# A decoder block in one kernel: five 512-column products ahead of the first scores, and transfers held to four at a time

## The chip, the cores and the metric

The kernel runs on one core of a Trainium2 chip. A core has TensorE (PE in the profile; its weight loads are listed apart as PEld), VectorE (DVE), ScalarE (ACT), GpSimd (POOL), SyncE (SP), and 16 DMA engines between HBM and the on-chip memories SBUF and PSUM. The metric is the device time of one execution in microseconds; lower is better.

## The reference, cut to what matters

Chunked attention: 4 batches, 8 heads, 768 positions, head size 64. Each chunk of 32 queries sees 8 memory keys, the 16 positions on its left, itself and 8 on its right. The attention output, 3072 tokens of 512 numbers, goes through a two-layer network with a rational function between the layers.

```
scores = scale * np.matmul(q_c, k_full.transpose(0, 1, 3, 2))
scores = scores - np.max(scores, axis=-1, keepdims=True)
a = np.exp(scores)
a = a / (np.sum(a, axis=-1, keepdims=True) + 1e-09)
out[:, :, c_start:c_end] = np.matmul(a, v_full)
...
h = x @ w_in                                  # 512 -> 2048
P = a[0] + a[1] * h + a[2] * h2 + a[3] * h3
Q = 1.0 + np.abs(b[0]) * np.abs(h) + np.abs(b[1]) * h2
return ((P / (Q + 1e-06)) @ w_out)            # 2048 -> 512
```

The weights arrive as 64-bit floats; the kernel unpacks them to 32-bit ones itself.

## The kernel before

The 3072 tokens are six blocks of 512. For each block the attention of four head pairs is computed, then the two layers. Each large product is made of three matmuls, since every operand is split into a high and a low part. The order of the work at the start is written out by hand in the string `SEQ`, one token per step, and the scheduler is told to keep it (`pin`, and `keep_in_program_order` for the loads).

What matters here is the first 30 us. All loads go out on one queue, SyncE's, in the order of the program, through the helper `load`. Load 1 is a part of the weights (512 KB). Loads 2 and 3 bring queries and keys of head pair 0 of block 0 (token `q00`, two halves of 288 KB), loads 4 and 5 those of pair 2 (`q02`), 6 and 7 those of pair 1 (`q01`), 8 and 9 the values of pair 0 (`v00`, two halves of 256 KB), 10 and 11 `q03`, 12 weights, 13 the 24 bytes of parameters, 14 and 15 `v02`, 16 and 17 `v01`, 18 weights, 19 and 20 `q10`, 21 and 22 `v03`. The framework gives the loads eight semaphores in turn, `DMAHW0` to `DMAHW7`, so a load waits for the landing of the eighth ahead of it.

TensorE begins, in `begin`, with `WARM` products that nobody reads: 14 transposes of the 128x128 identity matrix (`warm_up`). Then, as `SEQ` has it, come the scores of pair 0 and pair 2 (`b00`, `b02`, in `att_scores`, 16 matmuls each on 32-column strips of the array), the transpose of the exponentials of pair 0 (`c00`, in `att_turn`), the scores of pair 1 (`b01`), the values of pair 0 (`d00`, in `att_values`), the scores of pair 3 (`b03`), and the transposes `c02` and `c01`, one after the other. Between scores and transposes a pair passes through VectorE (`att_max`, `att_less`), ScalarE (`att_exp`) and a small fill on GpSimd (`absent`). A 32-bit matmul of the program, unlike a transpose, stands in the trace as two MATMUL records: the 16 of one `att_scores` are 32 there.

Of the kernel before, what the change touches and what calls it, by code (L numbers as in the profile page):

```python
# [35 lines left out]
SUMS_PE = [(0, 0), (0, 2), (1, 0), (1, 1), (1, 2)]  # L36
HI_ACT = [3, 4, 6, 10, 11, 12, 13, 15, 17, 18, 20, 22, 23, 25]
XL_POOL = [(0, 0), (0, 2), (1, 0), (1, 1), (1, 2)]
WARM = 14
CLEAR = [("qk", 0, "vp"), ("qk", 3, "ap"), ("qk", 1, "pv"), ("qk", 2, "vv"), ("v", 1, "pa"), ("v", 2, "pv"), ("v", 0, "pp"), ("v", 3, "pp")]  # L40
LEAD = 22
WHEN = dict(b=0, m=1, x=2, c=2, z=3)
WAIT = 4
# [46 lines left out]
def attn_moe(ctx, tc, qk, vm, w, ab, out, seq):  # L90
    nc = tc.nc
    P = 128
# [26 lines left out]
    ident = const.tile([P, P], F32, name="ident")  # L119
# [21 lines left out]
    def pin(ins):  # L141
        if pinned[0]:
            tc.keep_in_program_order(ins)

    def load(dst, src, queue=nc.sync):
        ins = queue.dma_start(out=dst, in_=src)
        if in_order[0]:
            tc.keep_in_program_order(ins)

# [5 lines left out]
    def slot(s, name, dtype, words=4 * DM):  # L155
        qk_bufs.pop(s, None)
        return wp.tile([P, 4 * DM], dtype, name=name, tag=f"slot{s}")[:, :words]
# [4 lines left out]
    def w_load(kind, j):  # L162
        if kind == "in":
            raws[j] = slot(RAW_SLOTS[j], "w_raw", U32)
        if j < WHOLE:
            load(half(raws[j], kind), half(w_bits_of[j][:, :4 * DM], kind))
        elif kind == "in":
            load(raws[j], w_bits_of[j][:, :4 * DM])
# [49 lines left out]
    def clear(region, engine):  # L218
        if engine is nc.scalar:
            engine.copy(region, zero.broadcast_to(region.shape))  # L220
        else:
            engine.memset(region, 0.0)

    def load_qk(i, p, t, queue=nc.sync):
        u = unit.setdefault((i, p), {})
        u["q"], u["k"] = [], []
        for h in range(2):
            load(rows(t[:, h * NK:h * NK + NK + NQ], h), qk[i, p, h], queue)
        for c in range(NC):
            u["q"].append(t[:, NK + c * CHUNK:NK + (c + 1) * CHUNK])  # L230
            first = t[:, start_in(c):start_in(c) + KEYS]
            u["k"].append(bass.AP(first.tensor, first.offset, [list(first.ap[0]), [NK + NQ, 2], [1, KEYS]]))
# [392 lines left out]
    def plan(n, kind, i, p):  # L625
        att.setdefault((n, kind), []).append((i, p))

    units = [(i, p, base) for i in range(3, NBLK)
             for p, base in enumerate(BASES.get(i, [first[i] - LEAD + 4 * p for p in range(NPAIR)]))]
    went = []  # L630
# [28 lines left out]

    warm = ps_h.tile([P, 512], F32, name="warm", tag="h")  # L660

    def warm_up():
        pin(nc.tensor.transpose(out=warm[:, :P], in_=ident, identity=ident))  # L663

    def begin():
        pick = {"a": nc.scalar, "v": nc.vector, "p": nc.gpsimd}
        for name, n, who in CLEAR:
            engines = [pick[x] for x in who]
            if name == "qk":
                t = qk_bufs[QK_SLOTS[n]] = slot(QK_SLOTS[n], "qk", F32, 2 * NK + NQ)  # L670
                clear(t[:, :NK], engines[0])
                clear(t[:, NK + NQ:], engines[1])
            else:
                if n >= 2:
                    v_bufs[n] = slot(V_SLOTS[n - 2], "v_first", F32).rearrange("x (h n) -> x h n", h=2)
                for h in range(2):
                    clear(v_bufs[n][:, h], engines[h])
        for _ in range(WARM):
            warm_up()
        if SUMS_PE:  # L680
            pin(nc.vector.tensor_reduce(ones, ident.rearrange("p (w h) -> p h w", h=2), axis=AX.X, op=ALU.max))

# [10 lines left out]
    def hand(token):  # L693
# [11 lines left out]
        elif kind in single:  # L705
            if kind == "o":
                early[0] = False
            single[kind](following(kind))
        elif kind in convert:
            convert[kind](w_seq[done[kind]])  # L710
            done[kind] += 1
        elif kind == "q":
            att_load(i, p)
        elif kind == "v":
            if i < BLOCKWISE:
                load_v(i, p, v_bufs[p if i == 0 else p % 2])
            else:
                att_loadv(i, p)
        elif kind == "E":
            evac(*order[count["o"]], [int(where)])  # L720
        elif kind == "K":
            fetch()
        elif kind == "X":
            ps_early.close()
            ps_pairs.append(ctx.enter_context(tc.tile_pool(name="ps_pairs", bufs=1, space=bass.MemoryType.PSUM)))
        elif kind == "W":
            warm_up()
        elif kind == "Y":
            load(par[:1], ab)
        elif kind == "P":  # L730
            wide = warm[:, P:P + 6]
            pin(nc.tensor.matmul(wide, lhsT=lone, rhs=par[:1], start=True, stop=True))
            pin(nc.scalar.copy(par, wide))
            pin(nc.scalar.activation(bab, par[:, 4:6], AF.Abs))
        previous[0] = kind

    pinned[0] = True
    tc.cur_priority = 900
    begin()
    for token in SEQ.split():  # L740
        tc.cur_priority += 4
# [102 lines left out]
```

## Time and profile before

| | |
|---|---|
| median of 3 runs | 599.34 us (598.25 to 599.51) |
| profiled execution, its own time | 598.73 us |
| its span in the trace | 596.9 us, so 1.8 us lie around it |
| PE busy | 586.8 us, 98% of the span |
| DVE, ACT, POOL busy | 78%, 67%, 68% |

The table says that TensorE is the engine that is nearly never idle; where its few idle times lie is read from the chain of waits and the timeline. Times below are from the start of the span.

### The profile page before, as it was taken

The numbers are of one execution on the slowest core, as the hardware profiler recorded it, in microseconds if no ns is written. First come the engines' busy times: TensorE is split into PE (matmuls) and PEld (weight loads), VectorE is DVE, ScalarE is ACT, GpSimd is POOL, SyncE is SP. The second block draws the span as 40 slices with busy tenths as digits, with TensorE's granted clock in tenths as the row PEclk, the third lists the DMA queues.
The fourth block names the chain that finished last, engine by engine and source line by source line (L and its number), as shares of the span: only waits on it lengthen the run. The fifth ranks groups of instructions, "written<-read, shape, count | busy, mean of one in ns | idle before, by whom it ended". The sixth has DMA issues, their size and how long they took to land.

```text
span 596.9 us, 13088 instructions
## 1 busy us (share of the span) xinstructions
PE 586.8 (98%) x5111; PEld 478.4 (80%) x5111; DVE 464.9 (78%) x762; ACT 401.9 (67%) x665; POOL 406.4 (68%) x376
## 2 busy tenths in 40 slices
PE   7899999999999999999999999999999999999997
PEld 6677888888787878878888888888888888888886
DVE  5899999898797759888877778787787766666673
ACT  4699999898667655656566666565765656755673
POOL 5468998798546766576677576766667677667682
PEclk9999999999999999999999999999999999999999
DMA  8965346230345344332331422312510100100001
GB/s 304 406 206 213 146 177 212 72 128 13 124 131 165 98 151 127 94 111 72 99 87 50 154 43 87 94 36 81 178 36 1 37 10 9 71 1 1 0 1 70
DMA packets 34591, 61.14 MB, mean 102 GB/s; under 512 B 4066, under 2 KB 20706, under 8 KB 34146
## 3 DMA queue, kind: packets, MB, share of 16 engines
q1 hardware_dynamic: 34386, 60.18, 30.6%
q8 instruction: 40, 0.66, 0.5%
q14 instruction: 21, 0.17, 0.1%
q10 hardware_dynamic: 144, 0.13, 0.1%
HBM read 44.56 MB, written 7.34 MB: 87 GB/s over the span
## 4 chain that ended last, share of the span: by engine, by line
PE 95%; DVE 2%; ACT 1%; DMA 1%; issue 0%; SPq 0%; POOL 0%; DVEq 0%
PE h L489 44%; PE o L504 43%; PE pairs L315 2%; PE pairs L293 2%; PE pa L428 1%; PE pa L361 1%; DMA qk<-in_qk_dram 1%; PE pa L412 1%; PE pa L454 0%; DVE e L379 0%; PE pa L434 0%; ACT e L396 0%; DVE ct L602 0%; ACT eT L419 0%; PE warm L663 0%
## 5 line engine op out<-in xcount | busy, mean ns | idle before, releaser
L489 PE MATMUL h<-x_hi,w_hl 128*128 128x512 f32 x768 | 240.3, 394 | 0.4 <-DVE ct L602 0.3
L504 PE MATMUL o<-w_hl,ghi 128*128 128x512 f32 x768 | 236.8, 390 | 0.0
L566 POOL TENSOR_TENSOR cy<-cy,ha 128x512 f32<-128x512 f32 x96 | 124.6, 1298 | 140.4 <-ACT cy L562 135.8
L504 PEld LDWEIGHTS o<-w_hl,ghi 128*128 128x128 f32 x768 | 143.9, 188 | 29.8 <-ACT v_main L546 0.2
L489 PEld LDWEIGHTS h<-x_hi,w_hl 128*128 128x128 f32 x768 | 141.7, 188 | 32.4 <-DVE ct L602 1.1
L489 PE MATMUL h<-x_lo,w_hl 128*128 128x512 f32 x384 | 150.0, 391 | 0.2 <-POOL x_lo L467 0.2
L504 PE MATMUL o<-w_hl,glo 128*128 128x512 f32 x384 | 150.0, 391 | 0.0
L614 POOL TENSOR_TENSOR glo<-ct,ghi 128x512 fp32r<-128x512 f32 x95 | 122.9, 1294 | 9.1 <-ACT ghi L609 3.2
L594 DVE SCALAR_TENSOR_TENSOR ct<-ct,par,h 128x512 f32<-128x512 f32 x82 | 61.2, 746 | 56.2 <-ACT h L590 55.5
L575 DVE TENSOR_TENSOR ct<-ct,h 128x512 f32<-128x512 f32 x96 | 65.6, 684 | 39.4 <-ACT ct L571 37.8
L586 ACT ACTIVATE h<-cy 128x512 f32<-128x512 f32 x82 | 49.1, 599 | 69.5 <-DVE ct L579 56.1
L557 ACT ACTIVATE ha<-h 128x512 f32<-128x512 f32 x96 | 57.4, 598 | 54.4 <-PE h L489 54.3
L607 POOL TENSOR_TENSOR ghi<-ct,zero 128x512 fp32r<-128x512 f32 x81 | 84.2, 1040 | 2.5 <-PE o L504 1.2
L504 PEld LDWEIGHTS o<-w_hl,glo 128*128 128x128 f32 x384 | 72.1, 188 | 16.8 <-POOL glo L614 1.6
L489 PEld LDWEIGHTS h<-x_lo,w_hl 128*128 128x128 f32 x384 | 72.1, 188 | 16.1 <-POOL x_lo L467 0.6
L562 ACT ACTIVATE cy<-ha,bab 128x512 f32<-128x512 f32 x96 | 78.4, 817 | 2.6
L571 ACT ACTIVATE ct<-h,par 128x512 f32<-128x512 f32 x96 | 73.6, 766 | 5.6 <-PE h L489 5.5
L579 DVE SCALAR_TENSOR_TENSOR ct<-ct,par,h 128x512 f32<-128x512 f32 x96 | 71.6, 746 | 3.0
L602 DVE SCALAR_TENSOR_TENSOR ct<-h,ct 128x512 f32<-128x512 f32 x82 | 56.5, 689 | 2.6
L598 DVE SCALAR_TENSOR_TENSOR h<-cy,h 128x512 f32<-128x512 f32 x82 | 56.5, 689 | 0.0
L590 ACT ACTIVATE h<-h 128x512 f32<-128x512 f32 x82 | 47.7, 582 | 2.6
L204 POOL TENSOR_TENSOR w_hl<-w_raw,w_hl 128x512 fp32r<-128x512 f32 x32 | 42.0, 1318 | 6.4 <-ACT w_hl L199 5.7
(80 smaller groups left out, 461.9 us busy)
## 6 DMA issues: line engine op xcount, KB each, us to landing
w_raw<-in_w_dram SPq DMA_DIRECT2D x26, 512.0 KB, 5.9
qk_pairs<-in_qk_dram SPq DMA_DIRECT2D x16, 576.0 KB, 4.2
v_main<-in_vm_dram SPq DMA_DIRECT2D x16, 512.0 KB, 5.1
out_dram<-v_main SPq DMA_DIRECT2D x23, 256.0 KB, 2.3
qk<-in_qk_dram SPq DMA_DIRECT2D x16, 288.0 KB, 5.8
eT<-blocks SPq DMA_DIRECT2D x64, 64.0 KB, 2.1
xf<-blocks SPq DMA_DIRECT2D x64, 64.0 KB, 2.1
v_main<-in_vm_dram SPq DMA_DIRECT2D x12, 256.0 KB, 6.4
```

The costliest lines, as they stand in the source:

```text
L489: pin(nc.tensor.matmul(h, lhsT=wt[:, cols], rhs=xt[i][:, ct, :], start=ct == m == 0, stop=ct == NCT - 1 and m == 2))
L504: ins = nc.tensor.matmul(o, lhsT=gt[:, cols], rhs=wt, start=begin and m == 0, stop=end and m == 2)
L557: pin(nc.scalar.activation(c["ha"], c["h"], AF.Abs))
L562: pin(nc.scalar.activation(c["y"], c["ha"], AF.Identity, scale=B1, bias=B0))
L566: pin(nc.gpsimd.tensor_tensor(c["y"], c["y"], c.pop("ha"), op=ALU.mult))
L571: pin(nc.scalar.activation(c["t"], c["h"], AF.Identity, scale=A3, bias=A2))
L575: pin(nc.vector.tensor_tensor(t, t, h, op=ALU.mult))
L579: pin(nc.vector.scalar_tensor_tensor(t, t, A1, h, op0=ALU.add, op1=ALU.mult))
L594: pin(nc.vector.scalar_tensor_tensor(t, t, A0, r, op0=ALU.add, op1=ALU.mult))
L598: pin(nc.vector.scalar_tensor_tensor(r, yy, QC, r, op0=ALU.add, op1=ALU.mult))
L607: pin(nc.gpsimd.tensor_tensor(ghi, chain[z]["t"], zero.broadcast_to([P, TB]), op=ALU.add))
L614: pin(engine.tensor_tensor(glo, chain.pop(z)["t"], gh[z].bitcast(F32), op=ALU.subtract))
```

## The change

The constant `WARM` goes from 14 to 5, and `begin` calls `warm_wide` in place of `warm_up`: a real 32-bit matmul of the identity with the identity repeated four times, 512 columns, into the same PSUM tile. The calls of `warm_up` that `SEQ` makes later (token `W`) stay. In `load`, each of loads 5 to 40 gets a dependency on the load four ahead of it, so that SyncE issues it only when that one has landed.

```diff
-WARM = 14
+WARM = 5
+AHEAD = 4
+PACED = 40
...
+    sent = []
+
     def load(dst, src, queue=nc.sync):
         ins = queue.dma_start(out=dst, in_=src)
+        sent.append(ins.ins)
+        if AHEAD < len(sent) <= PACED:
+            tc.add_manual_dep(ins.ins, sent[-1 - AHEAD].name, mybir.DependencyInfo(mybir.DependencyClass.Sync, mybir.DependencyReason.DATA), reason="pace")
...
+    def warm_wide():
+        pin(nc.tensor.matmul(warm.rearrange("p (b n) -> p b n", n=P), lhsT=ident, rhs=ident.unsqueeze(1).broadcast_to([P, 4, P]), start=True, stop=True))
+
...
         for _ in range(WARM):
-            warm_up()
+            warm_wide()
```

The first place is the start of TensorE's program, before and after the change; `warm` is the unread tile, `pa` a tile of scores, and the brackets name the semaphores waited for.

```order
L663 MATMUL warm<-ident 128x128 [waits Pool_49]
L663 MATMUL warm<-ident 128x128 x13
L361 MATMUL pa<-qk 32x128 [waits DMAHW1_49,DMAHW2_49,DVE_49,Pool_49]
L361 MATMUL pa<-qk 32x128 x15
L361 MATMUL pa<-qk 32x128 [waits DMAHW4_49,DMAHW3_49,DVE_49]
```

```order
L670 MATMUL warm<-ident 128x512 [waits Pool_49]
L670 MATMUL warm<-ident 128x512 x4
L368 MATMUL pa<-qk 32x128 [waits DMAHW1_49,DMAHW2_49,DVE_49,Pool_49]
L368 MATMUL pa<-qk 32x128 x15
L368 MATMUL pa<-qk 32x128 [waits DMAHW4_49,DMAHW3_49,DVE_49]
```

Nothing moved: the five wide products stand where the 14 transposes stood, and the scores behind them have the same waits. On all engines but SyncE the rest of the order and the waits are the same as before.

The second place is loads 4 to 16 in SyncE's program, before and after; `qk_120` is `q02`, `qk_117` is `q01`, `v_main0_102` is `v00`, `qk_114` is `q03`, `v_first_125` is `v02`, `v_main1_103` is `v01`.

```order
L146 DMA qk_120<-in_qk_dram 64x1152 [waits DVE_49] x2
L146 DMA qk_117<-in_qk_dram 64x1152 [waits Pool_49]
L146 DMA qk_117<-in_qk_dram 64x1152
L146 DMA v_main0_102<-in_vm_dram 64x1024 [waits Pool_49]
L146 DMA v_main0_102<-in_vm_dram 64x1024 [waits DMAHW0_49,Pool_49]
L146 DMA qk_114<-in_qk_dram 64x1152 [waits DMAHW1_49,Activation_49]
L146 DMA qk_114<-in_qk_dram 64x1152 [waits DMAHW2_49]
L146 DMA w_raw_148<-in_w_dram 128x1024 [waits DMAHW3_49]
L146 DMA par_93<-in_ab_dram 1x6 [waits DMAHW4_49]
L146 DMA v_first_125<-in_vm_dram 64x1024 [waits DMAHW5_49]
L146 DMA v_first_125<-in_vm_dram 64x1024 [waits DMAHW6_49,DVE_49]
L146 DMA v_main1_103<-in_vm_dram 64x1024 [waits DMAHW7_49]
```

```order
L150 DMA qk_120<-in_qk_dram 64x1152 [waits DVE_49]
L150 DMA qk_120<-in_qk_dram 64x1152 [waits DMAHW0_49,DVE_49]
L150 DMA qk_117<-in_qk_dram 64x1152 [waits DMAHW1_49,Pool_49]
L150 DMA qk_117<-in_qk_dram 64x1152 [waits DMAHW2_49]
L150 DMA v_main0_102<-in_vm_dram 64x1024 [waits DMAHW3_49,Pool_49]
L150 DMA v_main0_102<-in_vm_dram 64x1024 [waits DMAHW4_49,Pool_49]
L150 DMA qk_114<-in_qk_dram 64x1152 [waits DMAHW5_49,Activation_49]
L150 DMA qk_114<-in_qk_dram 64x1152 [waits DMAHW6_49]
L150 DMA w_raw_139<-in_w_dram 128x1024 [waits DMAHW7_49]
L150 DMA par_93<-in_ab_dram 1x6 [waits DMAHW0_49]
L150 DMA v_first_125<-in_vm_dram 64x1024 [waits DMAHW1_49]
L150 DMA v_first_125<-in_vm_dram 64x1024 [waits DMAHW2_49,DVE_49]
```

The order of the loads is the same; what moved is the semaphore waited for: load 5 now waits for load 1 (`DMAHW0`), where before the first load to wait for load 1 was load 9.

## Rows read from the trace of the kernel before

**Rows 1.** The page: busy time, and PE's granted clock in 40 slices (9: 90% or more).

```profile
PE 586.8 (98%) x5111; PEld 478.4 (80%) x5111; DVE 464.9 (78%) x762; ACT 401.9 (67%) x665; POOL 406.4 (68%) x376
...
PEclk9999999999999999999999999999999999999999
```

**Rows 2.** Whom TensorE's matmuls waited for, whole run: us, times, longest.

```profile
PE pa L361 <- DMA qk<-in_qk_dram: 2.0, 1, 2.0
...
PE pa L412 <- issue: 1.2, 1, 1.2
```

**Rows 3.** The chain that ended last, 0 to 18 us: start, us, what.

```profile
2.19 4.35 DMA qk<-in_qk_dram
...
8.67 0.70 DVE mx L369
...
10.98 0.66 PE pa L412 x4
...
16.34 1.13 issue
```

**Rows 4.** Timeline of the matmuls: start, us, line, out<-in, count, idle before.

```profile
1.44 3.25 PE L663 MATMUL warm<-ident 128*128 128x128 f32 x14 [1.44 <-POOL ident masks.py:199]
6.68 3.64 PE L361 MATMUL pa<-qk 128*32 128x128 f32 x64 [1.99 <-DMA qk<-in_qk_dram]
...
11.78 1.08 PE L361 MATMUL pa<-qk 128*32 128x128 f32 x32
...
17.47 0.60 PE L412 MATMUL pa<-ident,e 128*128 128x128 f32 x4 [1.20 <-issue]
...
18.43 1.08 PE L428 MATMUL pa<-v_first,eT 128*32 128x128 f32 x32
...
25.09 1.08 PE L428 MATMUL pa<-v_first,eT 128*32 128x128 f32 x32 [0.15 <-ACT eT L419]
```

**Rows 5.** Matmul groups, 1 to 10.5 us, then 10.9 to 20: busy us, mean ns.

```profile
L361 PE MATMUL pa<-qk 128*32 128x128 f32 x64 | 3.6, 420 | 2.0 <-DMA qk<-in_qk_dram 2.0
...
L361 PE MATMUL pa<-qk 128*32 128x128 f32 x64 | 2.2, 275 | 0.0
```

**Rows 6.** Packets, MB: 4-15, 15-15.1, 0-65.2, 65.2-66.3, 0-115.3, 115.3-116.4 us.

```profile
q1 hardware_dynamic: 1105, 3.92, 98.2%
...
q8 instruction: 1, 0.02, 62.8%
...
q8 instruction: 6, 0.10, 0.6%
...
q8 instruction: 1, 0.02, 5.2%
...
q8 instruction: 8, 0.13, 0.4%
...
q8 instruction: 1, 0.02, 5.5%
```

**Rows 7.** Busy us (and records) of PE, PEld, DVE, ACT, POOL in three stretches.

```profile
0.00:15.00 15.00, 10.91 (x202) 9.51 (x206) 8.31 (x15) 6.01 (x8) 8.21 (x21) 1.00 0.87 304
...
0.00:65.30 65.30, 59.07 (x839) 47.54 (x840) 56.03 (x101) 50.45 (x88) 42.04 (x58) 1.00 0.78 291
0.00:115.40 115.40, 109.17 (x1088) 88.68 (x1089) 101.81 (x174) 97.17 (x167) 86.02 (x93) 1.00 0.62 224
```

**Rows 8.** Issue to landing: loads 2 to 5; 15 to 17; 36 and 37.

```profile
DMA to landing us min/median/max: 4.3/4.4/4.4
...
DMA to landing us min/median/max: 6.7/6.7/6.8
...
DMA to landing us min/median/max: 2.9/2.9/2.9
```

**Rows 9.** Timeline of VectorE around 19 us.

```profile
18.25 0.68 DVE L324 TENSOR_REDUCE sums<-e 128x8 f32<-128x512 f32 x1
19.92 0.17 DVE L334 TENSOR_SCALAR rinv<-pa 128x8 f32<-128x8 f32 x1 [0.98 <-PE pa L434]
```

## The prediction

> **What bounds the kernel now.** I read the page first. TensorE is busy 98% of the span [rows 1], so whatever TensorE loses or wins early is likely to arrive at the end undiminished. Next, whom TensorE waits for over the whole run. Only two idle times there exceed 1 us: 2.0 us before the first scores, ended by the landing of queries and keys, and 1.2 us before a transpose, ended by nothing that the profile shows ("issue") [rows 2]. Both lie in the first 18 us, and both are on the chain that ended last [rows 3]. The two halves of the change aim at this stretch, so the question is what each does to these two places.
>
> The first place. Load 3 is issued at 2.19 and lands 4.35 later, at 6.54 [rows 3]. The scores of pairs 0 and 2 start at 6.68, 64 records that take 3.64 us [rows 4], and VectorE takes the maximum of the first pair from 8.67 [rows 3]. From there the chain runs through VectorE, ScalarE and GpSimd to the transpose at 10.98, so 2.31 us behind the maximum [rows 3]. In these early scores a record takes 420 ns on average, in the scores after 10.9 us only 275 [rows 5]; 32 of the later ones take 1.08 us, 64 of the early ones 3.64 [rows 4]. The page prints a granted clock of full speed in every slice [rows 1], but these durations say that the early scores ran at the lower level (1.2 GHz) and the later ones at the upper (2.4 GHz). The 14 transposes ahead of them, 3.25 us of work, with 1.99 us of idle time behind [rows 4], did not bring the clock up. It came up somewhere between 10.32, the end of the early scores (6.68 + 3.64), and 10.98, so 3.64 to 4.30 us after real matmuls began.
>
> The second place. From 16.34 TensorE stands for 1.13 us with all its inputs there [rows 3], and goes on at 17.47 [rows 4]. I read this as TensorE out of instructions, for these reasons. In 4 to 15 us the DMA engines carry loads alone, 1105 packets, 98% of their time; the first packet of 0.02 MB of queue 8, kind "instruction", starts between 15.0 and 15.1 [rows 6]. By then TensorE has 202 matmuls and 206 weight loads behind it, 408 records [rows 7]. The seventh packet starts at about 65.3 and the ninth at about 115.4 [rows 6], with 839 + 840 = 1679 and 1088 + 1089 = 2177 records done [rows 7]: a packet for each (2177 - 1679) / 2 = 249 records. At that pace the first one was due at 1679 - 6 x 249 = 185 records. TensorE gets there inside the scores that begin at 11.78, since 14 transposes, 64 scores, a transpose of four and two warm-up ones make 84 matmuls with as many weight loads, 168 records, ahead of them. So the packet was due at about 11.9 and began at 15.0, 3.1 us late, and TensorE went on 2.4 us after that, at 17.47. The loads issued at that time took 6.7 us from issue to landing; two alone on the queue took 2.9 [rows 8]. The 3.8 us between are queueing, near enough to 3.1 to be the same queue.
>
> **The wide products.** Removed are 14 transposes; 14 of them take 3.25 us, the last of them for some 0.42 after it started [rows 4, 5], so (3.25 - 0.42) / 13 = 0.217 us for 128 columns at the lower level. A real matmul stands as two records, as the 32 scores of a pair for the 16 of the program. How long a 512-column record of 32-bit data takes, no row shows. Upper bound: four times the 128-column transpose, 0.87 us; the scores support it, (3.64 - 0.42) / 15 = 0.215 for each round of four strips of 128 columns [rows 4, 5]. Lower bound: nothing, if the products ended before the queries land at 6.54. I take the upper bound, since the scores are the same kind of matmul. Five products are then 5 x 2 x 0.87 = 8.7 us at the lower level and end at 1.44 + 8.7 = 10.1 if the clock never comes up, and half of what is left goes once it does. With the clock up as long after the first real matmul as before, 3.64 to 4.30 us, it rises at 5.1 to 5.7, and the products end in the middle between that and 10.1: 7.6 to 7.9. That is later than the landing at 6.54, so the first scores now wait for their own warm-up instead of for data. They then run at the upper level: 1.08 us for 32 records [rows 4] and some 0.02 to VectorE, so the maximum begins at 8.7 to 9.0 instead of 8.67. **Term 1: +0.2 us** (0.0 to 0.3). The bounds are wider. With shorter products or an earlier clock, the maximum begins at 6.68 + 1.1 = 7.8: -0.9. If the clock does not rise until the products end, it begins at 10.1 + 1.1 = 11.2: +2.5. The scores of pair 2 behind them get faster too, but the transpose at 10.98 waits for the chain and not for them; that gain is nothing.
>
> **The pacing.** SyncE executes nothing but loads in this stretch, so what is queued behind a waiting load is the next loads alone. Loads 1 to 4 go as before. Load 5 now goes when load 1 has landed, and from there each fourth load follows a landing. A transfer alone takes 2.9 us [rows 8]; with 3 others ahead it took 4.4 in the bunch of loads 2 to 5 [rows 8]. So four in flight queue between 0 and 1.5 us, where eight queued 3.8. The instruction packet, due at 11.9 + 0.2, then begins at 12.1 to 13.6, and with the same 2.4 us behind it TensorE has its instructions by 14.5 to 16.0, before the 16.34 + 0.2 at which it needs them. The whole 1.13 us would go. What is late next is VectorE, which finishes its sum at 18.25 + 0.68 = 18.93 and idles for 0.98 until TensorE releases it at 19.92 [rows 9]; with TensorE earlier by more than that, VectorE sets the pace. **Term 2: -1.0 us** (0 to -1.1).
>
> What the pacing may cost: the landing of later loads. The tightest are the values `v02`, loads 14 and 15, read at 18.43 [rows 4], or at 18.43 - 1.1 + 0.2 = 17.5 after the change. Load 15 follows 11, 11 follows 7, and 7 follows 3, so it lands at 6.54 + 3 L, L being issue to landing with four in flight. At 2.9 it is 15.2, at 3.65 it is 17.5, at 4.4 it is 19.7. I take an L of 3.3, since the bunch of loads 2 to 5 started behind a load of twice the size and a steady flow of four does not bunch: cover of about 1 us, **term 3: 0** (0 to +3.7, below).
>
> The sum goes against the profiled execution's own 598.73: 598.73 + 0.2 - 1.0 = **597.9 us**. That execution is 0.6 below the median of the runs shown, 599.34; its clock came up just where the first transpose began, and a run with a later rise pays for it in the work from 10.98 on, which the change would spare. I do not add this.
>
> The Trainium skill, "DMA: Bandwidth & Descriptors", section "Queues, rings and completion order", says that a DMA engine goes round-robin over the queue rows it has work for, packet by packet. By that rule an instruction packet never waits behind the whole queue of loads, a shorter queue would not bring it sooner, and the sum would be that of rival B. The 3.1 us of delay above speak against it here, but they are inferred from counts.
>
> **The rivals.** A, the forecast: 597.9.
>
> B: the gap at 16.34 stays. The packet may be late for another reason than the loads' queue, or the idle time may be no lack of instructions at all. For it: the profile names no releaser for the gap, and only one execution is seen. Against it: delay and queueing agree (3.1 and 3.8). Time: 598.73 + 0.2 = 598.9.
>
> C: the pacing starves TensorE. For it: L was 4.4 when four were in flight [rows 8]. Then `v02` lands at 19.7 and TensorE waits 2.2 us for it; `v03`, load 22, follows load 2 (landed a transfer ahead of load 3, about 5.9) by five rounds, 5.9 + 5 x 4.4 = 27.9, where it is read at 25.09 [rows 4] - 1.1 + 0.2 + 2.2 = 26.4, another 1.5. Time: 597.9 + 3.7 = 601.6. It begins to cost at an L of 3.65, and decides the sign from about 4.1. Against it: 2.9 for a transfer alone, and that the DMA engines were nearly saturated by loads before as well, so that fewer in flight lose little.
>
> D: the first scores come with the data, from shorter products or an early clock: 598.73 - 0.9 - 1.0 = 596.8. It needs products that end by 6.7, so less than 5.2 us for the five.
>
> E: the clock rises only after the products: 598.73 + 2.5 - 1.0 = 600.2.
>
> **How the numbers follow.** A 0.50, B 0.20, C 0.10, D 0.14, E 0.06. I predict A's 597.9, with a range of its own of 597.2 to 598.6. A measurement of this kernel tells about 0.2%, 1.2 us, from no change: faster is below 598.1, slower above 600.5. Of A about two thirds lie below 598.1 (0.33), with D 0.47 faster; the rest of A, B, and E make 0.43; C makes 0.10. The range reaches from D's 596.8 to E, 600.0, and leaves out C, half of E and the edge of D.
>
> **What would show it.** Right: five products as ten records ending at 7.6 to 7.9, the maximum of pair 0 at 8.7 to 9.0; scores at the later duration (275 ns) from the start; loads 5 to 20 at 3 to 3.6 us from issue to landing; the first instruction packet by 13.6; no "issue" gap of 1 us around 16; `v02` landed before TensorE asks. Wrong: the gap is still there with its packet at 15 (B), TensorE waiting for a load between 12 and 26 us (C), products that take 5 us or 8.7 (D, E).

## The result and the profile after

The changed kernel takes 602.74 us, median of 8 runs (601.25 to 605.21), against 599.16 for the kernel before on the same chip: ratio 1.0058, 95% interval 1.0044 to 1.0073, so 3.5 us slower. The prediction was 597.9 us, in a range up to 600.0. The profiled execution took 602.7, with a span of 600.8 us.

The page of the profile after differs little from [rows 1]; what differs shows in whom TensorE's matmuls waited for over the whole run (us in total, times, longest), to be held against [rows 2]. (From `load` on, line numbers are 7 higher than before, from `warm_wide` on 10.)

```profile
PE 589.0 (98%) x5107; PEld 476.8 (79%) x5107; DVE 465.1 (77%) x762; ACT 401.8 (67%) x665; POOL 406.3 (68%) x376
```

```profile
PE pa L368 <- DMA qk<-in_qk_dram: 1.7, 2, 1.2
...
PE pa L435 <- DMA v_first<-in_vm_dram: 1.5, 2, 0.9
...
PE pa L435 <- DMA v_main<-in_vm_dram: 1.2, 2, 0.7
```

The reader is to see that the row with "issue" is gone, that the wait of 2.0 us ahead of the first scores is gone too, and that six waits for loads stand in their place, 4.4 us in all (1.7 + 1.5 + 1.2). The timeline of the matmuls after says where the early work and four of the six stand (compare [rows 4]):

```profile
1.44 6.49 PE L670 MATMUL warm<-ident 128*128 128x512 f32 x10 [1.44 <-POOL ident masks.py:199]
7.86 1.96 PE L368 MATMUL pa<-qk 128*32 128x128 f32 x64
11.31 0.66 PE L419 MATMUL pa<-ident,e 128*128 128x128 f32 x4 [1.50 <-POOL e L399]
...
16.01 1.40 PE L419 MATMUL pa<-ident,e 128*128 128x128 f32 x8
...
18.39 1.08 PE L435 MATMUL pa<-v_first,eT 128*32 128x128 f32 x32 [0.55 <-DMA v_first<-in_vm_dram]
...
20.83 1.08 PE L435 MATMUL pa<-v_main,eT 128*32 128x128 f32 x32 [0.73 <-DMA v_main<-in_vm_dram]
...
25.74 1.23 PE L368 MATMUL pa<-qk 128*32 128x128 f32 x32 [1.17 <-DMA qk<-in_qk_dram]
27.91 1.08 PE L435 MATMUL pa<-v_first,eT 128*32 128x128 f32 x32 [0.94 <-DMA v_first<-in_vm_dram]
```

The products run to 7.9 us and the 64 early scores behind them take 1.96 us, where they took 3.64. The transposes `c02` and `c01` run from 16.01 without the gap between them, behind which `c01` stood at 17.47. At the values `v02` nothing is left of that: 18.39 against 18.43. Then four waits for loads follow one another. VectorE's first maximum, in the timeline of that engine after, is 0.34 us later than in [rows 3]:

```profile
9.01 0.69 DVE L376 TENSOR_REDUCE mx<-pa 128x8 f32<-128x512 f32 x1 [4.23 <-PE pa L368]
```

The loads of the kernel after, grouped by time of issue (4 to 7 us, 13 to 14.5, 17 to 17.9, 18.5 to 20; the last column is us from issue to landing, as in [rows 8]):

```profile
qk<-in_qk_dram SPq DMA_DIRECT2D x3, 288.0 KB, 3.6
...
v_first<-in_vm_dram SPq DMA_DIRECT2D x2, 256.0 KB, 4.2
...
v_main<-in_vm_dram SPq DMA_DIRECT2D x2, 256.0 KB, 2.9
...
qk<-in_qk_dram SPq DMA_DIRECT2D x2, 288.0 KB, 5.9
```

Most loads land sooner than before, but fewer are on the way, and the flow stops twice. SyncE's timeline of the kernel after (start of the first load, us to the end of the last issue, number of loads):

```profile
13.07 1.82 SPq L150 DMA_DIRECT2D v_first<-in_vm_dram  x2
17.02 1.11 SPq L150 DMA_DIRECT2D v_main<-in_vm_dram  x2
18.18 0.59 SPq L150 DMA_DIRECT2D w_raw<-in_w_dram  x1
18.88 1.50 SPq L150 DMA_DIRECT2D qk<-in_qk_dram  x2
20.65 4.10 SPq L150 DMA_DIRECT2D v_first<-in_vm_dram  x2
```

Behind load 15 (issued at 14.4) nothing goes out until load 16 at 17.02: it waits for load 12, which is 512 KB of weights and took 5.2 us. Behind load 21 (20.65) load 22 goes only at 24.3: it waits for load 18, weights too, which took 6.0. After each stop the engines nearly stand still: from 17.2 to 18.2 us their busy share is 0.04, from 24.2 to 25.5 it is 0.16. The windows of both kernels, before first and after second, show what that makes of the flow (window; its length; busy us and records of PE, PEld, DVE, ACT, POOL; granted clock; DMA share; GB/s):

```profile
10.00:20.00 10.00, 8.14 (x223) 6.68 (x215) 7.43 (x15) 5.92 (x11) 1.60 (x4) 1.00 1.00 384
20.00:30.00 10.00, 9.62 (x131) 6.95 (x130) 9.25 (x20) 7.00 (x15) 5.40 (x7) 1.00 1.03 407
30.00:45.00 15.00, 14.44 (x299) 11.49 (x297) 14.66 (x27) 13.95 (x25) 9.18 (x12) 1.00 0.62 203
```

```profile
10.00:20.00 10.00, 8.00 (x215) 6.63 (x215) 7.84 (x16) 6.00 (x11) 1.61 (x4) 1.00 0.78 253
20.00:30.00 10.00, 7.16 (x119) 5.37 (x119) 6.69 (x16) 4.70 (x11) 3.60 (x4) 1.00 0.79 261
30.00:45.00 15.00, 13.66 (x198) 9.96 (x200) 14.09 (x24) 13.31 (x24) 9.36 (x14) 1.00 0.85 292
```

Between 10 and 30 us the loads come at 253 and 261 GB/s where they came at 384 and 407; after 30 us the paced kernel still brings what the other already has. Its TensorE, VectorE and ScalarE all do less in 20 to 30 us. As a mark for the whole start I take the first product of the second layer, before and after, from the timelines:

```profile
52.00 0.61 PE L504 MATMUL o<-w_hl,ghi 128*128 128x512 f32 x2
```

```profile
55.92 0.61 PE L511 MATMUL o<-w_hl,ghi 128*128 128x512 f32 x2
```

It starts 3.92 us later, and the span is 600.8 - 596.9 = 3.9 us longer. The loss is complete before the second layer begins.

### The profile page after: what moved, and what is told of

It is laid out like the page before. It is cut to its first block, busy times and chain, and to the rows that moved or that the text cites. A ratio compares the mean times of both kernels' runs of the same rounds, so it can differ in the third digit from the quotient of the medians.

```text
span 600.8 us, 13082 instructions
## 1 busy us (share of the span) xinstructions
PE 589.0 (98%) x5107; PEld 476.8 (79%) x5107; DVE 465.1 (77%) x762; ACT 401.8 (67%) x665; POOL 406.3 (68%) x376
## 4 chain that ended last, share of the span: by engine, by line
PE 91%; DMA 6%; POOL 1%; DVE 1%; ACT 1%; issue 0%; SPq 0%; POOLq 0%
PE o L511 43%; PE h L496 43%; DMA v_main<-in_vm_dram 2%; PE pairs L322 2%; DMA w_raw<-in_w_dram 2%; PE pairs L300 2%; DMA qk<-in_qk_dram 1%; DMA v_first<-in_vm_dram 1%; PE pa L435 1%; POOL v_main L229 0%; POOL qk L229 0%; POOL v_first L229 0%; PE pa L461 0%; PE pa L419 0%; PE pa L368 0%
```

## The experiments

The theory after this result: pacing at four makes the loads too slow, rival C of the prediction. Against it stood two others: that the wide products cost the time (a late first chain), and that the paced flow is tied to the slowest of the 16 DMA engines. Each kernel is the changed kernel with the edit shown; ratios are to the kernel before on the same chip. Its medians there run from 598.76 to 599.21 us, so kernels of different experiments are best compared by their ratios.

**The products alone.**

```diff
-PACED = 40
+PACED = 0
```

> Wide products alone, no pacing. Theory S (four loads in flight starve TensorE; the wide products cost 0.3 us): within 0.5 us of before, about 599.4, with the gap of 1.1 us near 16 us still there and the first instruction packet at about 15. Rival W (the wide products cause the loss): above 601, and no wait of TensorE for loads after the first scores.

Measured: 599.4 us, ratio 1.0003 [0.9990, 1.0017]. That is what theory S had. The products by themselves cost nothing that can be told, so they do not explain the loss. TensorE's timeline of this kernel:

```profile
18.11 0.60 PE L461 MATMUL pa<-ident,xt 128*128 128x128 f32 x4 [1.25 <-DVE e L386]
```

A gap of 1.25 us is still there. It stands behind the transposes `c01`, where it stood ahead of them: four matmuls with their four weight loads later, 8 records. The change puts 5 products (10 matmul records and as many weight loads) where 14 transposes (28 records in all) stood, so exactly 8 fewer. A gap that keeps its place by the count of records is what a lack of instructions gives. The packet of queue 8 begins at 15.7 us, TensorE goes on 2.4 later, as before. The row names an instruction of VectorE, but in the changed kernel the same transposes run at 17.24, ahead of that instruction (17.41 there), so they do not need it.

**The pacing alone.**

```diff
-WARM = 5
+WARM = 14
...
-            warm_wide()
+            warm_up()
```

> Pacing alone, 14 transposes. Theory S: slower by 3 us or more, about 602.4 (the changed kernel less 0.3), TensorE waiting 4 to 5 us in all for loads between 17 and 45 us, no 1 us gap near 16. Rival W: within 1 us of before, or faster by the 1.0 of the gap.

Measured: 601.33, ratio 1.0039 [1.0027, 1.0051], so 2.3 us of the 3.5. The direction is that of theory S; its 602.4 us and its 4 to 5 us of waits were too high. The waits for loads:

```profile
PE pa L368 <- DMA qk<-in_qk_dram: 3.4, 3, 2.0
...
PE pa L435 <- DMA v_first<-in_vm_dram: 0.8, 1, 0.8
PE pa L435 <- DMA v_main<-in_vm_dram: 0.7, 2, 0.5
```

The 2.0 is the wait ahead of the first scores, as in [rows 2]; the other 2.9 us are new. The first product of the second layer stands at 54.17.

**Which loads.**

```diff
-PACED = 40
+PACED = 12
```

> Wide products, but only loads 5 to 12 wait for the fourth ahead. Theory S with the fetch reading (an instruction packet late behind eight queued loads): the gap near 16 us is gone or under 0.4 us, TensorE waits for no load after the first scores, time 598.2 to 598.9, so 0.3 to 1.0 under before. Rival F (the gap closed for another reason, or the loads 13 and later refill the queue in time to delay the packet): gap still 1 us, about 599.4.

Measured: 599.71, ratio 1.0012 [1.0002, 1.0023]. Paced up to load 12, it loses little (0.1 to 1.4 us by the interval); most of the loss lies in loads 13 to 40. The gap near 16 us is gone, as expected of S, but against it TensorE waits 0.86 us for `v02` at 18.95, and the time did not fall.

**How many in flight.** Three kernels with `AHEAD` of 6, 3 and 5 in place of 4.

```diff
-AHEAD = 4
+AHEAD = 6
```

> As the changed kernel, but each load waits for the sixth ahead. If the loss is that four in flight do not cover the latency of a load (3 to 4 us fixed, so six at 0.8 us each cover 4.8): the loss is gone, 598.5 to 599.5. If the loss is that any wait on a landing ties all engines to the slowest one: half or more of the loss stays, above 600.5.

Measured: 598.79, ratio 0.9997 [0.9984, 1.0010]: the loss is gone, as the first reading has it.

```diff
-AHEAD = 4
+AHEAD = 3
```

> As the changed kernel, with three loads in flight instead of four. Theory L (a load takes 4 to 5 us from issue to landing whatever the queue, so n in flight give n loads in that time; measured: four gave one load per 1.24 us): one load per 1.4 to 1.6 us, the loss grows by 5 us or more, 607 or above. Rival B (the DMA engines' bandwidth is the limit and pacing only shifts a few waits): under 604.

Measured: 608.31, ratio 1.0157 [1.0130, 1.0184], as theory L has it.

```diff
-AHEAD = 4
+AHEAD = 5
```

> Five wide products, five loads in flight, between four (602.7) and six (598.8). If n in flight give n loads per 5 us, five give one per 1.0 us, so load 34 lands about 7 us sooner than with four and only the wait for the values of pair 2 is left: 599 to 600.5. If the loss comes from the tie to the slowest engine whatever the number: 601 or more.

Measured: 599.63, ratio 1.0007 [0.9996, 1.0018], as expected in time, though what TensorE still waits for is 0.7 us of queries and keys and not the values of pair 2. So with the five products: three in flight +1.6%, four +0.6%, and from five on no difference that can be measured, up to the eight that the semaphores allow anyway. The windows of 20 to 30 us go with it; those with five, and with three, in flight:

```profile
20.00:30.00 10.00, 9.74 (x129) 6.96 (x130) 9.01 (x18) 6.72 (x14) 5.38 (x7) 1.00 0.98 345
```

```profile
20.00:30.00 10.00, 8.14 (x147) 6.39 (x147) 5.42 (x13) 4.55 (x12) 1.34 (x2) 0.83 0.73 235
```

345 GB/s are enough here; 303 (the pacing alone) and 261 (the change) are not.

**What the closed gap is worth.** The 14 transposes with six in flight: pacing loose enough not to starve TensorE.

```diff
-AHEAD = 4
+AHEAD = 6
-WARM = 5
+WARM = 14
...
-            warm_wide()
+            warm_up()
```

> 14 transposes, six loads in flight. If pacing by six alone closes the gap near 16 us: 597.9 to 598.6, with the first maximum at 8.7 as before. If six leave the packet late: 598.9 to 599.4.

Measured: 599.54, ratio 0.9999 [0.9988, 1.0010]. The packet begins at 13.5 us and TensorE's timeline shows the gap closed:

```profile
16.33 0.66 PE L419 MATMUL pa<-ident,e 128*128 128x128 f32 x4 [0.22 <-POOL e L399]
...
17.80 1.08 PE L435 MATMUL pa<-v_first,eT 128*32 128x128 f32 x32 [0.37 <-ACT eT L426]
...
51.52 0.62 PE L511 MATMUL o<-w_hl,ghi 128*128 128x512 f32 x2
```

Against [rows 4] the transposes `c01` are 17.47 - 16.33 = 1.14 us earlier; 0.17 of it is an earlier start (the first transposes stand at 10.81, against 10.98), the rest is the gap. The values behind them are 18.43 - 17.80 = 0.63 earlier, as they now wait for ScalarE's copy of the transposes. The second layer begins 0.48 earlier (52.00 - 51.52), and the median shows nothing; by the interval a gain is under 0.7 us. The gap closes and the time does not fall, so neither forecast holds.

**Shorter products, with and without pacing.**

```diff
-AHEAD = 4
+AHEAD = 6
-WARM = 5
+WARM = 3
```

> Three wide products instead of five, and six loads in flight. If the reading of both terms holds, the products end by 6.7 us, the first maximum begins at 7.8 instead of 8.7 and the gap near 16 us is under 0.5: 597.0 to 598.2, so 0.6 to 1.8 under before. Rival: the gain of the early scores is lost on VectorE or ScalarE or to a late clock: within 0.5 us of before, 598.3 to 599.3.

Measured: 597.47, ratio 0.9972 [0.9962, 0.9983], as the first reading has it: the products end at 5.7 us, the maximum begins at 7.87 and the gap is 0.23.

```diff
-PACED = 40
+PACED = 0
-WARM = 5
+WARM = 3
```

> Three wide products and no pacing: which of the two edits carries the gain of the kernel with three products and six loads in flight (1.7 us). If both do: the first maximum at 7.8 as there, the 1.1 us gap near 16 back, 598.0 to 598.7. If the clock alone: 597.5. If the pacing alone: 599.2.

Measured: 597.44 (597.03 to 597.89), ratio 0.9964 [0.9951, 0.9977], the fastest kernel of this study together with the one before it, and 1.6 us below the kernel before (2.2 by the ratio). Its timeline of TensorE:

```profile
6.91 1.08 PE L368 MATMUL pa<-qk 128*32 128x128 f32 x32 [0.70 <-POOL v_main L229]
...
10.36 0.66 PE L419 MATMUL pa<-ident,e 128*128 128x128 f32 x4 [0.87 <-POOL e L399]
...
24.05 0.74 PE L368 MATMUL pa<-qk 128*32 128x128 f32 x19 [0.78 <-issue]
```

Three products end at about 6.2 us, so the scores come with the data, and at full speed (the row names a fill on GpSimd, but load 3 lands at 6.77, 0.14 ahead of the scores, as in the kernel before); the first transposes stand 0.62 us ahead of those of before. The gap that was forecast near 16 us is not there, although eight loads are in flight: the packet begins at 14.3 us, and 2.4 later, at 16.7, TensorE still has work. A gap without a releaser stands at 24.05 instead, 2.4 us behind the second packet (21.7). So it is not shown that the gain is that of the early scores alone. The second layer begins 0.47 earlier than before, less than the medians differ; the two profiled executions themselves differ by 0.84, since that of before was 0.4 below its median and this one 0.45 above. No pacing is needed for the gain.

```diff
-WARM = 5
+WARM = 3
```

> Three wide products with the pacing of the change (four in flight to load 40). It asks what sets the time of the paced kernel. Theory 'loads': between 18 and 45 us TensorE waits for loads, so an earlier start is only waited away; the first product of the second layer begins where it does with five products and four in flight, 55 to 56 us (within 0.5 of 55.9), waits for loads add up to 5 to 6 us instead of 4.4, and the time is 602 to 603. Theory 'start': the loss of the pacing (2.3 us, measured with 14 transposes) and the gain of three products (1.6, measured without pacing) add up: 599.0 - 1.6 + 2.3 = 599.7, ratio 1.001.

Measured: 600.84, ratio 1.0034 [1.0019, 1.0049]. It lies between the two theories and bears out neither's numbers. The second layer begins at 54.27, as with the 14 transposes and four in flight (54.17), though the first transposes stand 0.45 us earlier (10.55 against 11.00): under this pacing an earlier start is waited away (its waits for loads are 3.9 us, against 2.9). In this execution the clock came up late, as the 64 early scores take 2.39 us, against 1.96 in the changed kernel. But it does not begin at 55.9 either.

**The slowest DMA engine.** A load is spread over the 16 engines (load 35 of the kernel before, alone on its way, keeps them busy to 0.93 from 34 to 35 us), and a paced load waits until the last of them is through. The probe adds five transfers of 16 KB, in one piece and read by nobody, behind loads 12, 16, 20, 24 and 28; the second kernel has the same without pacing.

```diff
+PROBES = [12, 16, 20, 24, 28]
...
+        if len(sent) in PROBES and len(probed) < len(PROBES):
+            n = len(probed)
+            probed.append(dr.tile([1, 4093], F32, name=f"probe{n}"))
+            extra = nc.sync.dma_start(out=probed[n], in_=qk[5, n % 4, n // 4].rearrange("d n -> (d n)")[:4093].unsqueeze(0))
```

> The changed kernel with five extra transfers of 16 KB from HBM to HBM that nobody reads, each in one piece, on SyncE's queue behind loads 12, 16, 20, 24 and 28. They stand for what an instruction packet does to one DMA engine. Theory K (a wait for a landing ties all sixteen engines to the slowest one, so 16 KB more on one engine, the time of about a load on it, delays the loads behind it): slower than the changed kernel by 2 to 5 us, 604.5 to 607.5. Rival L (only the latency of a load counts, the engines have room): within 1 us of it.

Measured: 603.76, ratio 1.0084 [1.0063, 1.0106], 1.0 us above the changed kernel, with intervals that overlap (1.0063 to 1.0073).

```diff
-PACED = 40
+PACED = 0
```

> The same five extra transfers with the five wide products and no pacing (eight loads in flight). Theory K: the loads queued behind each other absorb it, slower than the kernel with wide products alone by under 1.5 us, 599 to 600.5. Rival: the probes cost as much here as in the paced kernel, so they say nothing on pacing.

Measured: 599.57, ratio 1.0001 [0.9991, 1.0012]: without pacing the probes cost nothing that can be told. In the paced kernel the direction is that of K, but the size is not, and the difference is not clear of noise: the probes do not show K. The trace of the changed kernel itself says more. These are its DMA engines from 17.2 to 18.2 us, in 40 slices:

```profile
GB/s 164 0 0 0 0 0 164 0 0 0 0 0 164 0 0 0 0 0 164 0 0 0 0 0 0 0 0 0 0 0 0 0 0 0 0 0 0 0 0 0
DMA packets 8, 0.02 MB, mean 16 GB/s; under 512 B 4, under 2 KB 4, under 8 KB 8
```

Four packets of 4 KB go through one after the other, as on one engine, 16 KB in all, a sixteenth of a load of 256 KB; then nothing moves until the loads issued at 17.02 and 17.60 begin to. Load 15 lands at 18.3 and `v02` is taken at 18.39. So here a landing waits for one engine's part while the others have nothing to do, as K has it. Which engine lags, and whether the instruction packet of 13.9 us held it up, the trace does not tell; nor does it tell what share of the loss this is.

The profiled execution with probes and pacing shows one long wait and then a thing that nobody expected, in the timeline of TensorE and in its windows:

```profile
23.80 1.94 PE L442 MATMUL pa<-v_main,eT 128*32 128x128 f32 x32 [3.06 <-DMA v_main<-in_vm_dram]
```

```profile
22.50:26.00 3.50, 2.20 (x34) 1.84 (x35) 0.00 (x0) 0.64 (x1) 0.00 (x0) 0.50 0.72 260
26.00:30.00 4.00, 4.00 (x21) 3.19 (x23) 2.62 (x5) 1.44 (x4) 0.00 (x0) 0.59 0.89 267
```

The granted clock (the column ahead of the last two) is 0.50 and 0.59: after the wait the 32 matmuls for the values take 1.94 us where they took 1.08. (The probe adds 7 lines: L442 is L435 of the change.)

## Why the prediction was wrong, step by step

**Term 1 was right, in part by luck.** Forecast were ten records ending at 7.6 to 7.9 and a maximum at 8.7 to 9.0; measured 7.9 and 9.01, and +0.2 us without pacing. But the same ten records differ from one execution to the next. In those with the products alone and with six in flight:

```profile
1.44 5.98 PE L670 MATMUL warm<-ident 128*128 128x512 f32 x10 [1.44 <-POOL ident masks.py:199]
1.44 7.34 PE L670 MATMUL warm<-ident 128*128 128x512 f32 x10 [1.44 <-POOL ident masks.py:199]
```

The maximum begins at 8.50 and at 9.87 there. One of these records takes 0.59 to 1.22 us in the changed kernel, so what differs is when the clock came up; the prediction took one value, 3.64 to 4.30 us, from one execution. Rival D, scores that come with the data, needs products of 5.2 us; three of them take 4.25 to 5.49, five take 5.98 at the least.

**Term 2 had the right mechanism and the wrong size.** The gap is a lack of instructions: it moves by exactly the 8 records that the program was shortened by. The packet mostly comes sooner with a shorter queue: with 14 transposes at 12.8 us (four in flight) and 13.5 (six) in place of 15.0 [rows 6], with five products at 13.9 (four), 13.7 (five) and 14.5 (six) in place of 15.7. With three products it begins at 12.7 (four), but at 14.4 with six, against 14.3 with eight, so six do not always help. With only three loads in flight (and five products) it begins at 12.7, with 92 + 96 = 188 records done, next to the 185 at which the prediction had it due. The forecast for four was 13.6 at the latest. The Trainium skill, "DMA: Bandwidth & Descriptors", section "Queues, rings and completion order", has each engine go round-robin over the queue rows, packet by packet. By that alone a shorter queue would not have brought the packet sooner; these rows show that with four in flight it did. But the 1.13 us counted at their full length as -1.0 are worth at most 0.5 at the second layer and nothing that the runs can tell. VectorE, which I named as next, was not the first to be late with the gap closed and six in flight: it was ScalarE's copy of the transposes.

**Term 3 is the step that failed:** "I take an L of 3.3, since the bunch of loads 2 to 5 started behind a load of twice the size and a steady flow of four does not bunch". Loads 7, 11 and 15, each issued as the one before it landed, took 3.8, 3.7 and 3.8 us, so load 15 landed at 18.3 and not at 16.4, and TensorE waited for `v02`. The chain of load 22 took 4.4 a round (from 5.9, the landing of load 2, to 27.8 in five), because load 18 in it, 512 KB of weights, took 6.0, and loads 19 and 20 beside it 5.9. A flow that mixes 256, 288 and 512 KB does bunch, and where one engine lags, as from 17.2 us on, L lasts until that one is through. The bound of 3.65, from which it begins to cost, was near the mark. That of 4.1 for the sign does not follow from the prediction's own sums: 5.9 + 5 L for load 22 against 25.09 - 1.1 + 0.2 uses up the 0.8 us of gain at an L of 3.8. Rival C's 601.6 us and its +3.7 for the loads were close to the 602.74 and to 4.4 us of waits, and the chance of 0.10 was far too low. The argument against C, "that the DMA engines were nearly saturated by loads before as well, so that fewer in flight lose little", had it backwards: the engines were saturated because eight were queued, and with four their share fell from 1.00 to 0.78.

C's nearness is in part chance: it had `v02` at 19.7, and it was followed no further than `v03`. Of the waits, the two for `v02` and `v03` are 0.55 + 0.94; the others are for `v01`, for queries and keys, and for loads that are read after 30 us. A load issued late makes every later one late.

**What stays open.** Pacing at four costs 2.3 us behind the transposes, but 602.74 - 599.4 = 3.3 behind five products and 600.84 - 597.44 = 3.4 behind three (by the ratios 3.3 and 4.2). By the intervals the first difference is not clear of noise, the second barely. For three, a start that is earlier and is waited away accounts for some of it; five do not start earlier (11.31 against 11.00 us for the first transposes). In the profiled execution of the changed kernel the loads of 20 to 30 us came at 261 GB/s, with pacing alone at 303. Why they were slower there I could not settle. The lag of a single DMA engine is one candidate (it is seen at work from 17.2 us on, but not measured against the kernel with pacing alone), stretches at the lower clock another: of the eight runs of the changed kernel the two slowest (604.26 and 605.21) have a mean granted clock of 0.997, the other six 0.999 or 1.0. Neither is shown to be the cause.

## What to carry to other kernels

Before holding transfers back, multiply out the flow: loads in flight times their size over issue to landing must come near the rate at which the unpaced kernel brings them at its busiest stretch (345 GB/s to its 407 were enough here, 303 were not), for every load that is paced and not just for the next to be read. A place taken by a large load is free only when its slowest part has landed. A gap that is closed is worth what is left of it at the next wait of every engine behind it, not its length. Warm-up work pays if it brings the clock up and ends when the data land, not 1.3 us later (7.86 against 6.54): a kernel with just that, without any pacing, gained 1.6 us here.

## What the runs showed of the hardware beside that

The granted clock can fall back at the start of a run. With probes and pacing TensorE stood 3.06 us for a load and had little work around it (0.75 us of 2.5 busy from 20 to 22.5 us); from 22.5 to 26 us the clock was at half, the lower level (1.2 GHz), and by 30 us it was back. With three in flight it happened too, after 0.89 of 2.5 us busy, and a window of 22.5 to 26 us in which the engine was busy throughout ran at 0.56:

```profile
22.50:26.00 3.50, 3.50 (x77) 2.67 (x69) 1.76 (x6) 0.00 (x0) 0.62 (x1) 0.56 0.86 270
```

So a wait for a load can cost more than its length. How much of the +1.6% with three in flight is this, no run separates.

The 64 early scores take 3.64 us behind 14 transposes [rows 4], at the lower level, and 1.96 behind five products, at the upper (2.4 GHz). The Trainium skill, "TensorE: Matmul & The Clock Gate", "Part 4: PE-mode transpose", says that a transpose does not bring the full clock. The trace agrees, but the transposes were also the shorter work, 3.25 us against 6.49 and with an idle time behind it, so no run here tells the two apart.
